# A squared-ReLU attention and mixer kernel: residual transposes moved in SyncE's queue, and two more x transposes on TensorE

## The chip, the cores and the metric

One NeuronCore of a Trainium2 chip runs the whole program. Five engines work beside each other and meet at semaphores: TensorE (PE in the profile; its weight loads are PEld), VectorE (DVE), ScalarE (ACT), GpSimd (POOL) and SyncE (SP), which here only issues DMAs. The metric is the device time of one execution in microseconds, the median over runs.

## The reference

```python
scores = scale * np.matmul(q, k.transpose(0, 1, 3, 2))      # q, k, v: 8 x 12 x 448 x 64
attn = np.maximum(scores, 0.0) ** 2 / S
attn_out = np.matmul(attn, v)
x = attn_out.transpose(0, 2, 1, 3).reshape(B, S, H * D)     # 8 x 448 x 768
xt = x.transpose(0, 2, 1)
h = np.maximum(xt @ w_tok1, 0.0) @ w_tok2                   # 448 -> 256 -> 448
u = x + h.transpose(0, 2, 1)
h2 = np.maximum(u @ w_ch1, 0.0) @ w_ch2                     # 768 -> 1536 -> 768
return u + h2
```

All inputs and the output are float32; the kernel computes in bfloat16 with float32 accumulation.

## The kernel before, in words

The 96 heads are taken in 24 groups of four (`ND`), three groups (`DB`) to a batch of the eight. For one group the work is:

- `load_four` brings q, k and v by DMA from GpSimd's queue (four buffers for each name); `transposes` turns q and k on TensorE (L141) and copies them to `qkT` (L155).
- `scores` multiplies for one of seven chunks of keys (L165); ScalarE applies ReLU into `at` (L174), and VectorE squares it (L181).
- `values` multiplies with v (L193); `values_out` scales the result into `xT` (L211), which has the model's channels on the partitions.
- `x_back` turns `xT` into `x_sb`, tokens on the partitions. It has two ways. For groups below `XDMA` it makes eight TensorE transposes into a PSUM buffer of the pool `ps_mm` (tag `bank`, two buffers; L237) and a copy (L246). From `XDMA` on it issues two DMA transposes on SP's queue (L229).
- `token1` and `token2` are the two token-mixing products (L255 with ReLU in L263, L278); VectorE adds `xT` and writes `uT_sb` (L286).
- `u_back` issues two DMA transposes on SP's queue that turn the group's part of `uT_sb` into `u_sb`, the residual with tokens on the partitions (L308). `u_sb` has three buffers, one for a batch.

When a batch's three groups are through, `channel_work` puts its channel mixing into a queue of units: twelve `channel1` units (six matmuls each, L320, with ReLU in L327) and two `channel2` units (twelve matmuls each, L359) for each output tile of 128 rows. The second of each pair of batches has four tiles, the first three; tiles are numbered t=0 to 6 over a pair. A `channel2` unit covers half of the 768 columns; VectorE adds `u_sb` to its result into `out_sb` (L366), and after the second half SP issues two DMAs to the output (L378). The `channel2` units of batch 0 are queued only with those of batch 1. All units take their PSUM from the same two `bank` buffers as `token1` and the TensorE form of `x_back`.

Groups 0 to 2 and the step of group 3 have a schedule written out by hand. From step i = 4 on, one loop holds the order: in step i, `scores` belong to group i, while `values`, `x_back`, `token1` and `token2` belong to group i-1, and `transposes` to group i+1. `fill` takes units from the queue by a credit of estimated cost. In each step, behind `x_back(i-1)`, comes the load of group i+3; if group i-1 is not below `XDMA`, a one-element GpSimd copy (`gate`, L537) that reads `x_sb` stands ahead of it in GpSimd's queue, so that the load waits until the DMA transposes have landed.

The order of the code is the order in each engine's queue; each queue runs in order, and semaphores hold an instruction until its operands are there.

Of the kernel before, what the change touches and what calls it, by code (L numbers as in the profile page):

```python
# [16 lines left out]
def kernel(  # L17
# [20 lines left out]
    DB = H // 4  # L38
# [78 lines left out]
    def load_wc2(i, parts):  # L117
        n = EC // parts
        nc.gpsimd.dma_start(
            out=wc2[:, i * n : (i + 1) * n, :],  # L120
            in_=moe_w_ch2.rearrange("(e p) n -> p e n", p=128)[:, i * n : (i + 1) * n, :],
        )
# [36 lines left out]
    def scores(i, c):  # L159
        sb = qkT[i]  # L160
        ps = ps_att.tile([128, 2, 512], FP32, tag="att", name="sc_ps")
        for r in range(2):
            for g in range(2):
                h = slice(64 * g, 64 * (g + 1))
                nc.tensor.matmul(  # L165
                    ps[64 * r : 64 * (r + 1), g, :S],
                    lhsT=sb[h, r, 1, c * 64 : (c + 1) * 64],
                    rhs=sb[h, r, 0, :],
                    start=True,
                    stop=True,  # L170
                    skip_group_check=True,
                )
        at = attn.tile([128, 2, S], BF16, name="at", bufs=12)
        nc.scalar.activation(at, ps[:, :, :S], AF.Relu)  # L174
        squares.append(at)
        at2[i, c] = at

    def square(keep=0):
        while len(squares) > keep:
            at = squares.pop(0)  # L180
            nc.vector.tensor_tensor(out=at, in0=at, in1=at, op=ALU.mult)  # L181

    def values(i, cs):
        v_raw = raws[i, "v"]
        if i not in accs:
            accs[i] = [ps_acc.tile([128, 512], FP32, tag=f"acc{r}", name="acc_ps") for r in range(2)]
        ps = accs[i]
        for c in cs:
            at = at2.pop((i, c))
            for r in range(2):  # L190
                for g in range(2):
                    h = slice(64 * r, 64 * (r + 1))
                    nc.tensor.matmul(  # L193
                        ps[r][64 * g : 64 * (g + 1), :S],
                        lhsT=v_raw[h, g, c, :],
                        rhs=at[h, g, :],
                        start=(c == 0),
                        stop=(c == QC - 1),
                        skip_group_check=True,
                    )  # L200

    def values_out(i, split=False):
        b, d = divmod(i, DB)
        ps = accs.pop(i)
        for r in range(2):
            if split and r == 1:
                nc.scalar.activation(
                    xT[b % 2][:, 2 * d + r, :S], ps[r][:, :S], AF.Copy, scale=float(alpha2)
                )
                continue  # L210
            nc.vector.tensor_scalar(  # L211
                out=xT[b % 2][:, 2 * d + r, :S],
                in0=ps[r][:, :S],
                scalar1=float(alpha2),
                scalar2=None,
                op0=ALU.mult,
            )


    x_tiles, r1_tiles, uT_tiles = {}, {}, {}  # L220
    XDMA = 6

    def x_back(i, place="bank", copy=None):
        b, d = divmod(i, DB)
        x_sb = mix.tile([128, 2, 4, 128], BF16, name="x_sb")
        x_tiles[i] = x_sb
        if i >= XDMA:
            for r in range(2):
                nc.sync.dma_start_transpose(  # L229
                    out=x_sb[:, r], in_=xT[b % 2][:, 2 * d + r, :]  # L230
                )
            return
        pool = ps_mm if place == "bank" else ps_acc
        ps = pool.tile([128, 2, 512], BF16, tag=place, name="x_ps")
        for r in range(2):
            for c in range(4):
                nc.tensor.matmul(  # L237
                    ps[:, r, c * 128 : (c + 1) * 128],
                    lhsT=xT[b % 2][:, 2 * d + r, c * 128 : (c + 1) * 128],
                    rhs=ident,  # L240
                    is_transpose=True,
                    start=True,
                    stop=True,
                    skip_group_check=True,
                )
        (copy or nc.vector.tensor_copy)(  # L246
            x_sb.rearrange("n r c d -> n (r c d)"), ps.rearrange("n r t -> n (r t)")
        )
# [17 lines left out]
    def token2(i, early=False, rs=(0, 1)):  # L266
        b, d = divmod(i, DB)
        if d == 0 and b % 2 == 0 and 0 in rs:
            uT_tiles[b // 2] = mix.tile([128, NP, 2 * S], BF16, name="uT_sb")
        r1 = r1_tiles[i]  # L270
        off = (b % 2) * S
        if early:
            parts = {r: ps_mm.tile([128, 512], FP32, tag="bank", name="h_ps1") for r in rs}
        else:
            parts = {r: ps_acc.tile([128, 512], FP32, tag=f"acc{r}", name="h_ps") for r in rs}
        for r in rs:
            for j in range(JC):
                nc.tensor.matmul(  # L278
                    parts[r][:, :S],
                    lhsT=r1[:, j, r * 128 : (r + 1) * 128],  # L280
                    rhs=wt2[:, j, :],
                    start=(j == 0),
                    stop=(j == JC - 1),
                )
        for r in rs:
            nc.vector.tensor_tensor(  # L286
                out=uT_tiles[b // 2][:, 2 * d + r, off : off + S],
                in0=parts[r][:, :S],
                in1=xT[b % 2][:, 2 * d + r, :S],
                op=ALU.add,  # L290
            )
        if 1 in rs:
            u_back(i)


    r2_tiles, u_tiles, out_tiles = {}, {}, {}

    def chunks(b):
        half = NT // 2
        return range(half) if b % 2 == 0 else range(half, NT)  # L300

    def u_back(i):
        b, d = divmod(i, DB)
        t = chunks(b)
        if d == 0:
            u_tiles[b] = mix.tile([128, NP, NT - NT // 2, 128], BF16, name="u_sb", bufs=3)
        for p in (2 * d, 2 * d + 1):
            nc.sync.dma_start_transpose(  # L308
                out=u_tiles[b][:, p, : len(t), :],
                in_=uT_tiles[b // 2][:, p, t.start * 128 : t.stop * 128],  # L310
            )
# [91 lines left out]
    def fill(share, least=0):  # L403
        if not queue:
            return
        credit[0] += share * rate[0]
        done = 0
        while queue and (credit[0] > 0 or done < least):
            cost, unit = queue.pop(0)
            credit[0] -= cost  # L410
            unit()
            done += 1
# [74 lines left out]
    i = DB  # L487
    square()
    values(i - 1, (4, 5, 6))
    values_out(i - 1, split=True)  # L490
    scores(i, 0)
    token2(i - 2, early=True)
    x_back(i - 1, place="acc0")
    scores(i, 1)
# [4 lines left out]
    square(keep=1)  # L499
    scores(i, 3)  # L500
    token2(i - 1, early=True)
    square(keep=1)
    scores(i, 4)
# [15 lines left out]
    for i in range(DB + 1, ND + 2):  # L519
        slow = i <= 2 * DB  # L520
        if i == 2 * DB + 1:
            rate[0] = (EC * C1 + NT * C2) / DB
        if i < ND:
            scores(i, 0)
            scores(i, 1)
        if 0 <= i - 1 < ND:
            values(i - 1, range(QC))
            values_out(i - 1)
        if i < ND:
            scores(i, 2)  # L530
        if slow:
            fill(1 / 3, least=1)
        if 0 <= i - 1 < ND:
            x_back(i - 1)
        if i + PRE < ND:
            if i - 1 >= XDMA:
                nc.gpsimd.tensor_copy(gate, x_tiles[i - 1][:1, 1, 3, 127:])  # L537
            load_four(i + PRE)
        if i == 5:
            load_wc2(1, 2)  # L540
        square()
        if not slow:
            fill(1 / 3)
        if i < ND:
            scores(i, 3)
            scores(i, 4)
        if i + 1 < ND:
            transposes(i + 1)
        square()
        if not slow:  # L550
            fill(2 / 9)
        if 0 <= i - 1 < ND:
            token1(i - 1)
        fill(1 / 3 if slow else 1 / 9, least=1)
        if i < ND:
            scores(i, 5)
            scores(i, 6)
        if 0 <= i - 1 < ND:
            token2(i - 1)
            if (i - 1) % DB == DB - 1:  # L560
                channel_work((i - 1) // DB)
        square()
        fill(1 / 3, least=1 if slow else 0)
# [32 lines left out]
```

## Time and profile before

| | |
|---|---|
| median of 13 runs | 386.4 us (383.56 to 392.57) |
| the profiled execution | 386.83 us, span 385.1 us |
| TensorE busy | 366.2 us (95%) |
| VectorE, ScalarE, GpSimd busy | 205.4, 213.2, 98.0 us |
| mean granted TensorE clock | 0.994 |
| DMA moved | 43.84 MB, mean 114 GB/s |
| `u_sb` transposes on SP's queue | 48, median 3.3 us to landing (2.3 to 13.0) |
| `x_sb` transposes on SP's queue | 36, median 2.4 us to landing (2.4 to 9.4) |
| `x_sb` by TensorE | 6 groups |

The span runs from the first to the last instruction; the time of the run lies a little above it. A row of the timeline gives the start, the duration, the engine, the line, the operation with its output and input, and in square brackets the idle time of the engine before it with what ended it. "SPq" rows are issues on SP's queue and not transfers; the transfer lands later. Busy time of TensorE is modelled, so the idle between its groups is the better guide.

### The profile page before, as it was taken

Reading aid. Unit: us, or ns where it says so; the run is one execution under the profiler, and the core shown is the slowest. Engines: PE = TensorE matmul, PEld = TensorE weight load, DVE = VectorE, ACT = ScalarE, POOL = GpSimd, SP = SyncE. Lnnn points to the kernel's source line nnn. Section 1 sums busy time; section 2 is a strip of 40 time slices with the busy share of each in tenths; the row PEclk is TensorE's granted clock in tenths of the full one; section 3 lists DMA queues with packets and bytes.
Section 4 is the critical chain, followed back from the end, with each engine's and each line's share of the span. In section 5 each row is a group of like instructions: output and inputs, shape, how many; then the busy total and the mean of one; then the engine's idle time right before and its main releaser. Section 6 shows DMA issues by size and latency. Waiting matters only on the chain.

```text
span 385.1 us, 10117 instructions
## 1 busy us (share of the span) xinstructions
PE 366.2 (95%) x4319; PEld 200.0 (52%) x4319; DVE 205.4 (53%) x369; ACT 213.2 (55%) x297; POOL 98.0 (25%) x176
## 2 busy tenths in 40 slices
PE   8888979959999999999999999999999999999995
PEld 3444535524555655555545655555555555555563
DVE  2785668842576665555654756545744755121022
ACT  4996868844653446764676455764576455411400
POOL 8973632603303303213214303213030000000000
PEclk9999999998999999999999999999999999999999
DMA  8999999996367897478566687467571433224024
GB/s 151 118 138 175 159 202 176 184 161 93 61 121 123 156 167 132 60 112 149 119 96 78 119 165 136 75 99 135 104 116 27 90 90 94 53 44 108 0 51 114
DMA packets 72014, 43.84 MB, mean 114 GB/s; under 512 B 46048, under 2 KB 68512, under 8 KB 71968
## 3 DMA queue, kind: packets, MB, share of 16 engines
q0 software_dynamic: 24416, 21.47, 40.2%
q1 hardware_dynamic: 47248, 21.28, 28.3%
q8 instruction: 34, 0.56, 0.6%
q10 hardware_dynamic: 304, 0.43, 0.4%
q14 instruction: 12, 0.10, 0.1%
HBM read 43.38 MB, written 11.01 MB: 141 GB/s over the span
## 4 chain that ended last, share of the span: by engine, by line
PE 81%; DMA 11%; POOL 3%; DVE 2%; ACT 2%; issue 1%; POOLq 0%; ACTq 0%
PE m_ps L359 28%; PE m_ps L320 26%; PE sc_ps L165 8%; PE acc_ps L193 7%; PE t_ps L255 5%; PE h_ps L278 4%; DMA wc<-in_moe_w_ch_dram 4%; DMA x_sb<-xT 3%; DMA k_raw<-in_k_dram 3%; PE qkT_ps L141 2%; ACT at L174 1%; POOL q_raw L83 1%; DVE at L181 1%; DMA wt<-in_moe_w_tok_dram 1%; POOL wt L96 1%
## 5 line engine op out<-in xcount | busy, mean ns | idle before, releaser
L174 ACT ACTIVATE at<-sc_ps 128x896 bf16<-128x896 f32 x168 | 145.1, 921 | 58.9 <-PE sc_ps L165 58.6
L320 PE MATMUL m_ps<-uT_sb,wc 128*128 128x448 bf16 x564 | 116.7, 355 | 2.4 <-DMA wc<-in_moe_w_ch_dram 2.2
L359 PE MATMUL m_ps<-wc,r_sb 128*128 128x384 bf16 x672 | 115.2, 326 | 0.0
L181 DVE TENSOR_TENSOR at<-at 128x896 bf16<-128x896 bf16 x168 | 97.3, 620 | 6.9 <-ACT at L174 6.9
L359 PEld LDWEIGHTS <-r_sb 128*128 128x128 bf16 x672 | 64.3, 98 | 45.6 <-issue 4.1
L327 ACT ACTIVATE r_sb<-m_ps 128x448 bf16<-128x448 f32 x94 | 51.1, 543 | 63.4 <-PE m_ps L320 62.9
L320 PEld LDWEIGHTS <-wc 128*128 128x128 bf16 x564 | 53.5, 98 | 52.9 <-issue 5.2
L366 DVE TENSOR_TENSOR out_sb<-m_ps,u_sb 128x384 f32<-128x384 f32 x56 | 31.1, 555 | 61.2 <-PE m_ps L359 60.2
L165 PE MATMUL sc_ps<-qkT 64*64 64x448 bf16 x672 | 52.7, 360 | 2.9 <-ACT at L174 2.3
L286 DVE TENSOR_TENSOR uT_sb<-h_ps,xT 128x448 bf16<-128x448 f32 x48 | 27.8, 618 | 47.6 <-PE h_ps L278 47.5
L211 DVE TENSOR_SCALAR xT<-acc_ps 128x448 bf16<-128x448 f32 x45 | 26.1, 619 | 37.3 <-PE acc_ps L193 37.3
L537 POOL COPY gate<-x_sb 1x1 bf16<-1x1 bf16 x14 | 3.2, 227 | 150.4 <-DMA x_sb<-xT 150.4
L193 PE MATMUL acc_ps<-at,v_raw 64*64 64x448 bf16 x672 | 38.6, 350 | 0.0
L83 POOL DMA_DIRECT2D q_raw<-in_q_dram x48 | 28.8, 611 | 18.2 <-DMA wc<-in_moe_w_ch_dram 13.0
L165 PEld LDWEIGHTS <-qkT 64*64 64x64 bf16 x672 | 15.6, 105 | 31.6 <-issue 27.6
L255 PE MATMUL t_ps<-x_sb,wt 128*128 128x256 bf16 x192 | 25.6, 277 | 6.4 <-DMA x_sb<-xT 5.7
L83 POOL DMA_DIRECT2D v_raw<-in_v_dram x48 | 29.4, 634 | 8.6 <-DMA wc<-in_moe_w_ch_dram 5.7
L155 DVE COPY qkT<-qkT_ps 128x896 bf16<-128x896 bf16 x39 | 22.5, 618 | 15.9 <-PE qkT_ps L141 15.9
L83 POOL DMA_DIRECT2D k_raw<-in_k_dram x46 | 28.0, 625 | 3.1 <-DMA q_raw<-in_q_dram 2.4
L263 ACT ACTIVATE r_sb<-t_ps 128x512 bf16<-128x512 f32 x24 | 14.3, 597 | 25.5 <-PE t_ps L255 25.4
L193 PEld LDWEIGHTS <-v_raw 64*64 64x64 bf16 x672 | 20.2, 107 | 12.1 <-issue 0.8
L255 PEld LDWEIGHTS <-wt 128*128 128x128 bf16 x192 | 18.4, 99 | 12.3 <-DMA x_sb<-xT 5.2
(38 smaller groups left out, 118.8 us busy)
## 6 DMA issues: line engine op xcount, KB each, us to landing
out_dram<-out_sb SPq DMA_DIRECT2D x54, 192.0 KB, 2.7
q_raw<-in_q_dram POOLq DMA_DIRECT2D x48, 112.0 KB, 4.2
v_raw<-in_v_dram POOLq DMA_DIRECT2D x48, 112.0 KB, 5.2
k_raw<-in_k_dram POOLq DMA_DIRECT2D x46, 112.0 KB, 4.7
wc<-in_moe_w_ch_dram POOLq DMA_DIRECT2D x4, 1152.0 KB, 13.2
u_sb<-uT_sb SPq DMA_TRANSPOSE x48, 3.3
x_sb<-xT SPq DMA_TRANSPOSE x36, 2.4
k_first<-in_k_dram SPq DMA_DIRECT2D x1, 224.0 KB, 3.5
```

The costliest lines, as they stand in the source:

```text
L83: eng.dma_start(out=dst[64 * r : 64 * (r + 1)].rearrange("p g c d -> p g (c d)"), in_=src[b, h0 : h0 + 2].rearrange("g (p c) d -> p g (c d ...
L165: nc.tensor.matmul(ps[64 * r : 64 * (r + 1), g, :S], lhsT=sb[h, r, 1, c * 64 : (c + 1) * 64], rhs=sb[h, r, 0, :], start=True, stop=True, s ...
L174: nc.scalar.activation(at, ps[:, :, :S], AF.Relu)
L181: nc.vector.tensor_tensor(out=at, in0=at, in1=at, op=ALU.mult)
L193: nc.tensor.matmul(ps[r][64 * g : 64 * (g + 1), :S], lhsT=v_raw[h, g, c, :], rhs=at[h, g, :], start=(c == 0), stop=(c == QC - 1), skip_gro ...
L211: nc.vector.tensor_scalar(out=xT[b % 2][:, 2 * d + r, :S], in0=ps[r][:, :S], scalar1=float(alpha2), scalar2=None, op0=ALU.mult,)
L255: nc.tensor.matmul(ps[:, j, :], lhsT=wt1[:, c, j * 128 : (j + 1) * 128], rhs=x_sb[:, :, c, :], start=(c == 0), stop=(c == 3),)
L286: nc.vector.tensor_tensor(out=uT_tiles[b // 2][:, 2 * d + r, off : off + S], in0=parts[r][:, :S], in1=xT[b % 2][:, 2 * d + r, :S], op=ALU.add,
L320: nc.tensor.matmul(ps[:, :S], lhsT=wc1[:, g, e * 128 : (e + 1) * 128], rhs=uT[:, g, off : off + S], start=(g == 0), stop=(g == CC - 1),)
L327: nc.scalar.activation(r2[:, e, off : off + S], ps[:, :S], AF.Relu)
L359: nc.tensor.matmul(ps[:, :HN], lhsT=r2[:, e, t * 128 : (t + 1) * 128], rhs=wc2[:, e, cols], start=(e == 0), stop=(e == EC - 1),)
L366: nc.vector.tensor_tensor(out=o[:, cols].rearrange("n (g d) -> n g d", d=128), in0=ps[:, :HN].rearrange("n (g d) -> n g d", d=128), in1=u_ ...
```

## The change

Three things are edited. `XDMA` goes from 6 to 8, so groups 6 and 7 (steps 7 and 8) are transposed on TensorE, and the loads of groups 10 and 11 have no gate ahead of them. `token2` no longer calls `u_back`, but puts the group on a list. And from step 7 on, the loop takes from this list behind `x_back(i-1)`: one group in step 7, up to two in each later step.

```diff
     x_tiles, r1_tiles, uT_tiles = {}, {}, {}
-    XDMA = 6
+    XDMA = 8
...
         if 1 in rs:
-            u_back(i)
+            u_later.append(i)
...
     r2_tiles, u_tiles, out_tiles = {}, {}, {}
+    u_later = []
...
         if 0 <= i - 1 < ND:
             x_back(i - 1)
+        if i > 2 * DB:
+            for _ in range(1 if i == 2 * DB + 1 else 2):
+                if u_later:
+                    u_back(u_later.pop(0))
         if i + PRE < ND:
```

The list thus gives group 0 in step 7, groups 1 and 2 in step 8, 3 and 4 in step 9, 5 and 6 in step 10, 7 and 8 in step 11, 9 and 10 in step 12, and one group in each step after that. In SP's queue, the transposes of `u_sb` for group i-2 now come behind those of `x_sb` for group i-1, where before they came ahead of them.

## The prediction

> **What bounds the kernel now.** I read the page first: engine shares, slices.
>
> ```profile
> PE 366.2 (95%) x4319; PEld 200.0 (52%) x4319; DVE 205.4 (53%) x369; ACT 213.2 (55%) x297; POOL 98.0 (25%) x176
> ...
> DMA  8999999996367897478566687467571433224024
> ```
>
> TensorE is busy for 366.2 of 385.1 us; no other engine passes 55%. A change pays where TensorE idles, and costs where it adds TensorE work or a new wait. The DMA engines are full for the first nine slices of 9.6 us. Next, the table of waits.
>
> ```profile
> POOL gate L537 <- DMA x_sb<-xT: 150.4, 14, 12.5
> DVE out_sb L366 <- PE m_ps L359: 60.2, 30, 15.0
> PE t_ps L255 <- DMA x_sb<-xT: 5.7, 2, 4.8
> ```
>
> The gate's 150 us is GpSimd pacing loads; nobody computing waits for it. TensorE waits twice for a DMA transpose of x, 5.7 us in all. No DVE wait for `u_sb` appears: every `u_sb` was early. The timeline shows the long wait, in step 7. (Steps are known by their two `xT` evictions on DVE: 76.16 in step 7, 97.34 in 8, 112.05 in 9, 126.29 in 10.)
>
> ```profile
> 75.95 0.36 PE L165 MATMUL sc_ps<-qkT 64*64 64x448 bf16 x4
> 76.16 1.16 DVE L211 TENSOR_SCALAR xT<-acc_ps 128x448 bf16<-128x448 f32 x2 [1.20 <-PE acc_ps L193]
> 76.84 4.68 SPq L229 DMA_TRANSPOSE x_sb<-xT  x2
> 86.86 1.66 PE L255 MATMUL t_ps<-x_sb,wt 128*128 128x256 bf16 x8 [4.82 <-DMA x_sb<-xT]
> 88.32 2.39 PE L320 MATMUL m_ps<-uT_sb,wc 128*128 128x448 bf16 x6
> 90.64 0.57 PE L165 MATMUL sc_ps<-qkT 64*64 64x448 bf16 x8
> ```
>
> The first x transpose issues at 76.84, the pair lands at 86.8. The matmuls after the idle are slow: eight L255 in 1.66 us against 1.03 in step 9, six L320 in 2.39 against 1.31. The table of windows says why (busy columns, then granted clock 0.56):
>
> ```profile
> 86.80:90.70 3.90, 3.83 (x18) 1.92 (x22) 0.00 (x0) 0.60 (x1) 3.72 (x7) 0.56 0.63 73
> ```
>
> Last, step 10, where the put-off transposes will matter:
>
> ```profile
> 126.29 1.16 DVE L211 TENSOR_SCALAR xT<-acc_ps 128x448 bf16<-128x448 f32 x2 [1.27 <-PE acc_ps L193]
> 126.98 2.88 SPq L229 DMA_TRANSPOSE x_sb<-xT  x2
> 128.97 0.55 DVE L366 TENSOR_TENSOR out_sb<-m_ps,u_sb 128x384 f32<-128x384 f32 x1
> 131.37 2.12 PE L359 MATMUL m_ps<-wc,r_sb 128*128 128x384 bf16 x12
> 134.38 2.11 PE L359 MATMUL m_ps<-wc,r_sb 128*128 128x384 bf16 x12
> ```
>
> The DVE row at 128.97 is the second half of output tile t=3, the first tile of batch 1 (the `out_sb` rows run t=0 at 104.08 and 106.91, t=1 at 110.22 and 114.72, t=2 at 117.43 and 121.15, t=3 at 124.47 and 128.97).
>
> **What the Trainium skill says.** "TensorE: Matmul & The Clock Gate", Part 1, says that a whole idle window of about 3.4 us halves TensorE's clock, that a similar time of work restores it, and that the window runs freely. The trace agrees: after 4.82 us idle the clock was 0.56 for about 3.9 us; after 2.2 us idle at 51.8 six L320 still took 1.31. The same page (Architectural detail) calls DVE and ACT strict FIFO, so one late operand holds everything behind it on DVE. "DMA: Bandwidth & Descriptors", Issuing engines are not separate DMA queues, says that transfers of all issuers interleave on the same 16 engines; the x pair of step 7 took 8.3 and 9.4 us beside loads, 2.4 and 2.5 in step 8.
>
> **Part 1: PE transposes in steps 7 and 8.** Step 7: the model is the same operation in step 6 (xT ready at 67.68, x transposes 67.75 to 68.36, copy 68.40 to 69.09). Scores end at 76.31; the second xT is ready at 77.32. The first four transposes fit before it; the last four (half of 0.61) end at about 77.7. L320 x12, at 76.24 before, then starts 1.4 late. From there without the DMA wait: 2.4 (L320 x12) + 1.0 (scores and attention transposes) + 2.4 (L320 x12) + 1.0 (L255 x8) + 1.2 (L320 x6) = 8.0, so scores at 85.6 against 90.64: a gain of 5.0, of which about 1.7 is the cold clock (0.6 + 1.1). The x copy ends near 78.5, well before L255 at 83.4. Step 8: token1 had no wait there, so the 1.4 is pure cost. The two DVE copies (0.69 each) come out of DVE's idle (3.39 before the step 8 eviction; without that cover they would cost 1.4 in all).
>
> **Part 2: two gates fewer.** The loads of groups 10 and 11 no longer wait at 86.8 and 101.9, but follow the loads of group 9 (until 74.3), held only by their buffers. They meet the second half of `wc` in the full DMA time; it was issued at 69.05, the slowest `wc` landing took 18.0, and it is first needed at about 97. Worth nothing; if late, a microsecond or two.
>
> **Part 3: the residual transposes.** The built program shows that the six of batch 0 are not put off in time. They stand at the head of SP's queue, each waiting only for its own DVE add (issues from 25.18 to 40.0, as before). Only batch 1's six move: SP's order is now output t=0, x of group 8, u of groups 3 and 4, outputs t=1 and t=2, x of group 9, u of group 5, u of group 6. So the crowding up to 52 us stays; what leaves is the six transposes issued from 52.4 to 75.9. The `wc` wait that ends at 54.05 began at 51.8, before them, and from 54 to 76 TensorE was busy 21.78 of 22.0 us: worth nothing. In step 9 the wait of 0.83 (L255 at 118.13) should mostly vanish, since group 11's loads are no longer there: 0.6 (0 to 0.8).
>
> Step 9's new demand: t=3's first half (124.47) needs u of group 3 and half of 4. After x at 112.73, with 1.25 an issue, the third u transpose starts at 117.7; even at a landing of 5.2 (the u pair at 122.93) that is 122.9. In time, with a microsecond to spare.
>
> Step 10 is late. u of group 5 stands behind x of group 9: x issues 126.98 to about 129.6, its first u to 130.85, its second starts there and lands 2.3 (least) to 5.2 later. I take 2.8, the load of group 13 being gated still: 133.65. DVE wanted it at 128.97. Behind it in DVE's FIFO are t=4's first half, two qkT copies, two squares, and t=4's second half; TensorE has two `bank` buffers, filled with t=3 and t=4, and stops at 131.37. DVE then needs 0.05 + 0.56 + 0.56 + 1.15 + 1.15 + 0.56 = 4.0 until the buffer for t=5 is free, at 137.7; TensorE wrote t=5 at 134.38 before. Cost 3.3; bounds 2.8 and 5.7. TensorE's own idle there is 134.25 - 131.37 = 2.9, below the window; at landings over 3.4 us it can reach it, and adds up to 1.7.
>
> Later batches: u comes some 5 us later than before (from the end of a step to behind x in the next), but twelve `m_ps` L320 units (1.14 each, so 13.7 us) precede each batch's output tiles. Nothing.
>
> **Sum.** -5.0 + 1.4 - 0.6 + 3.3 = -0.9 us. Against the profiled execution (span 385.1, time 386.83) that is 385.9; it is 0.4 above the median of 386.4, so I predict 385.5 as the median. A change within 0.5% (1.9 us) can't be told from none: the forecast is "same", leaning to faster.
>
> **Rivals.** (1) The new stall hides: if the u of group 5 is early or DVE's wait doesn't reach TensorE, -5.0 + 1.4 - 0.6 = -4.2 gives 382.2. For: the wait is DVE's, which idles 2.2 us soon after; against: two buffers only, DVE in order. (2) Slower: the step 10 stall at its upper price plus a cold clock, 5.7 + 1.7, and nothing from step 9: +3.5, about 390. It decides (above 388.3) once the stall costs more than 6.1 with its cold clock, that is, a landing over about 4 us that also makes an idle window. For: u took 5.2 at 122.93; against: no loads are due at 131. (3) Step 7's stall in the trace is longer than usual, as a cold clock hangs on the window's phase: without it the gain is 3.3, and the sum +0.8, about 387.2. (4) The change doesn't do what it says: true of batch 0, but inside the likeliest case.
>
> **Chances.** Likeliest case 0.45 (its own range 384.5 to 387), hidden stall 0.22, slower 0.16, weaker gain 0.17. For 8 in 10 the range leaves out the far ends of (1) and (2): 382.7 to 388.6. Faster takes most of (1) and the lower edge of the likeliest: 0.30. Slower takes (2) and a little of (3): 0.19. Within: 0.51.
>
> **What would show it.** Right: no DMA wait before L255 in steps 7 to 9; an L237 group in steps 7 and 8 with about 1.1 us idle; no clock dip there; a new DVE wait for `u_sb` in step 10, of about 4.7 us, and a TensorE wait for `out_sb`'s buffer of about 3; u of batch 0 still issued from 25 us. Wrong: a DVE wait for `u_sb` at t=3's first half, a TensorE wait for `wc` or `k_raw` in steps 7 to 9, or no TensorE idle in step 10.

## The result, and the profile after

The changed kernel takes 388.28 us in the median (11 runs), the kernel before 385.88 in the runs beside it (48); the ratio is 1.0089, with a 95% interval from 1.0058 to 1.012. It is slower by 0.9%, some 3.4 us. This ratio leaves out slow runs, more than 1.5% above the fastest of the same kernel, and these are 14 of the 48 before and none after; the medians of all runs lie 2.4 us apart. The forecast was 385.5 us and no measurable change.

The page of the changed kernel, the shares and the DMA row as before, with the row of the granted clock:

```profile
PE 368.5 (95%) x4335; PEld 201.7 (52%) x4335; DVE 206.5 (53%) x371; ACT 213.1 (55%) x297; POOL 96.8 (25%) x174
...
PEclk9999999999999699999999999999999999999999
DMA  8999999941169939589367587549361254323023
```

The clock dips in one slice, the fourteenth (125 to 135 us). In the trace before, the dip was in the tenth. The table of waits (four of its rows):

```profile
DVE out_sb L367 <- PE m_ps L360: 62.1, 30, 15.0
DVE out_sb L367 <- DMA u_sb<-uT_sb: 5.5, 2, 5.2
PE m_ps L360 <- DVE out_sb L367: 3.5, 1, 3.5
PE t_ps L255 <- DMA x_sb<-xT: 1.5, 2, 1.1
```

The long DMA wait for x is gone, and two rows are new: VectorE waits 5.2 us for `u_sb` in step 10 (and once more, 0.28 us, in step 9, which TensorE doesn't feel), and TensorE 3.5 us for the VectorE operation that waited. Step 7 in the timeline:

```profile
73.95 1.15 DVE L211 TENSOR_SCALAR xT<-acc_ps 128x448 bf16<-128x448 f32 x2 [1.20 <-PE acc_ps L193]
74.64 0.93 PE L237 MATMUL x_ps<-ident,xT 128*128 128x128 bf16 x8 [0.53 <-DVE xT L211]
75.60 0.69 DVE L246 COPY x_sb<-x_ps 128x1024 bf16<-128x1024 bf16 x1 [0.49 <-PE x_ps L237]
...
81.03 1.04 PE L255 MATMUL t_ps<-x_sb,wt 128*128 128x256 bf16 x8
81.90 1.30 PE L321 MATMUL m_ps<-uT_sb,wc 128*128 128x448 bf16 x6
```

L255 follows without a wait, at the full clock (1.04 us for eight against 1.66). Step 10, where the time goes:

```profile
120.40 1.15 DVE L211 TENSOR_SCALAR xT<-acc_ps 128x448 bf16<-128x448 f32 x2 [1.09 <-PE acc_ps L193]
121.09 2.51 SPq L229 DMA_TRANSPOSE x_sb<-xT  x2
123.65 5.82 SPq L309 DMA_TRANSPOSE u_sb<-uT_sb  x4
128.39 1.02 DVE L367 TENSOR_TENSOR out_sb<-m_ps,u_sb 128x384 f32<-128x384 f32 x2 [5.23 <-DMA u_sb<-uT_sb]
129.00 4.00 PE L360 MATMUL m_ps<-wc,r_sb 128*128 128x384 bf16 x12 [3.45 <-DVE out_sb L367]
```

The u transposes of group 5 are issued at 123.65 behind x of group 9. VectorE, which had squared until 123.16, waits until 128.39; TensorE stops for 3.45 us. Twelve L360 then take 4.00 us instead of 2.11. The table of windows shows the clock. Its last three columns are the granted clock (0.52 in the first row), the DMA share and GB/s; ahead of them stand the busy times of PE, PEld, DVE, ACT and POOL:

```profile
128.90:134.80 5.90, 5.80 (x22) 3.23 (x22) 3.19 (x7) 0.00 (x0) 2.01 (x4) 0.52 1.13 199
134.80:141.00 6.20, 6.20 (x60) 3.25 (x62) 3.34 (x6) 2.98 (x4) 0.00 (x0) 1.00 0.26 69
```

From one `xT` eviction to the next the steps took (us):

| | before | after | difference | predicted |
|---|---|---|---|---|
| step 7 (76.16 / 73.95) | 21.18 | 15.88 | -5.30 | -5.0 |
| step 8 | 14.71 | 16.06 | +1.35 | +1.4 |
| step 9 | 14.24 | 14.51 | +0.27 | -0.6 |
| step 10 | 15.38 | 21.44 | +6.06 | +3.3 |
| sum | | | +2.38 | -0.9 |
| from there to the end of the span | 243.39 | 244.57 | +1.18 | 0 |

The two spans differ by only 1.3 (386.4 and 385.1), because step 7 came 2.2 us later in the trace before, after its `wc` wait. That wait, a long start, comes and goes between executions and isn't the change's: five of the thirteen traces of this case have it (1.85 to 3.54 us, with step 7 some 2 to 5.6 us late), and a second trace of the kernel before doesn't, with step 7's eviction at 74.08. From step 7 on the table gives +3.6 in all; against the second trace of the kernel before it is +2.7.

### The profile page after: what moved, and what is told of

It reads as the page before. It is cut to its first block, busy times and chain, and to the rows that moved or that the text cites. A ratio compares the mean times of both kernels' runs of the same rounds, so it can differ in the third digit from the quotient of the medians.

```text
span 386.4 us, 10103 instructions
## 1 busy us (share of the span) xinstructions
PE 368.5 (95%) x4335; PEld 201.7 (52%) x4335; DVE 206.5 (53%) x371; ACT 213.1 (55%) x297; POOL 96.8 (25%) x174
## 4 chain that ended last, share of the span: by engine, by line
PE 84%; DVE 6%; DMA 4%; ACT 3%; issue 1%; SPq 1%; POOL 0%; POOLq 0%; DVEq 0%; ACTq 0%
PE m_ps L360 27%; PE m_ps L321 26%; PE sc_ps L165 9%; PE acc_ps L193 8%; PE t_ps L255 6%; PE h_ps L278 5%; ACT at L174 3%; PE qkT_ps L141 2%; DMA x_sb<-xT 2%; DVE xT L211 2%; DVE at L181 1%; DVE uT_sb L286 1%; DMA q_raw<-in_q_dram 1%; DMA u_sb<-uT_sb 1%; PE m_ps L339 1%
## 5 line engine op out<-in xcount | busy, mean ns | idle before, releaser
L360 PE MATMUL m_ps<-wc,r_sb 128*128 128x384 bf16 x672 | 117.2, 330 | 3.5 <-DVE out_sb L367 3.5
L360 PEld LDWEIGHTS <-r_sb 128*128 128x128 bf16 x672 | 65.1, 99 | 50.0 <-issue 9.0
L542 POOL COPY gate<-x_sb 1x1 bf16<-1x1 bf16 x12 | 2.1, 177 | 140.8 <-DMA x_sb<-xT 140.8
L255 PE MATMUL t_ps<-x_sb,wt 128*128 128x256 bf16 x192 | 25.8, 279 | 2.2 <-DMA x_sb<-xT 1.5
L255 PEld LDWEIGHTS <-wt 128*128 128x128 bf16 x192 | 18.6, 100 | 8.5 <-issue 3.9
```

What stands on the lines that cost most here:

```text
L255: nc.tensor.matmul(ps[:, j, :], lhsT=wt1[:, c, j * 128 : (j + 1) * 128], rhs=x_sb[:, :, c, :], start=(c == 0), stop=(c == 3),)
L360: nc.tensor.matmul(ps[:, :HN], lhsT=r2[:, e, t * 128 : (t + 1) * 128], rhs=wc2[:, e, cols], start=(e == 0), stop=(e == EC - 1),)
```

## The experiments

Two theories stood against each other. A: the loss is the late u of group 5 in step 10 with the cold clock behind it. B: the TensorE transposes cost more than they save. A third (C) spreads the loss over all moved transposes.

**One part alone: the TensorE transposes.** The kernel before, with one line changed.

```diff
-    XDMA = 6
+    XDMA = 8
```

> Only the TensorE transposes of groups 6 and 7 (and so two gates fewer); the u transposes stay where they were before. Theory A (the loss is the late u of group 5 in step 10, with the cold clock that follows): no DVE wait for u_sb and no TensorE idle in step 10; step 7 takes about 16 us from xT to xT instead of 21, step 8 about 16 instead of 14.7; 4 us below before, ratio about 0.990. Theory B (the TensorE transposes cost more than they save, because the DMA wait of step 7 is usually short): ratio 1.00 or above.

Measured: 381.42 us (12 runs), ratio 0.9907 (0.9873 to 0.994). Step 7 took 15.88, step 8 16.06, step 10 15.22, no wait for `u_sb`, clock 0.998. B falls: this half of the change gains about 3.6 us. Once more, beside the gate experiment below:

> TensorE transposes of groups 6 and 7 alone, once more, beside the kernel with the gates kept: 381.4 again, ratio about 0.991, and 16 us from xT to xT in step 7.

381.06 us, ratio 0.9879 (0.984 to 0.9918), step 7 again 15.88.

**The other part alone: the put-off u transposes.** The changed kernel with `XDMA = 6`.

> Only the moved u transposes; x of groups 6 and 7 by DMA as before. Theory A: the late u of group 5 is there, DVE waits about 5 us for it in step 10 and TensorE about 3.5, with a cold clock after it; about 6 us above before, ratio about 1.015, less what the DMA wait of step 7 loses with the u of groups 4 and 5 out of its way (up to 5). Theory B: the moved transposes cost nothing, ratio 1.00 or below.

Measured: 387.66 us, ratio 1.0094 (1.0064 to 1.0123). The waits, longest first:

```profile
DVE out_sb L367 <- DMA u_sb<-uT_sb: 14.6, 3, 6.8
PE m_ps L360 <- DVE out_sb L367: 4.6, 1, 4.6
```

VectorE waits three times for `u_sb`: 6.77 us in step 8 (for t=0), 1.77 in step 9 and 6.04 in step 10. SP's queue in this kernel, against the changed one below it, says why:

```profile
74.51 3.56 SPq L229 DMA_TRANSPOSE x_sb<-xT  x2
78.11 2.56 SPq L309 DMA_TRANSPOSE u_sb<-uT_sb  x2
89.02 2.50 SPq L229 DMA_TRANSPOSE x_sb<-xT  x2
91.57 6.80 SPq L309 DMA_TRANSPOSE u_sb<-uT_sb  x4
```

```profile
0.74 0.76 SPq L83 DMA_DIRECT2D k_first<-in_k_dram  x1
25.37 16.13 SPq L309 DMA_TRANSPOSE u_sb<-uT_sb  x6
101.33 1.16 SPq L379 DMA_DIRECT2D out_dram<-out_sb  x2
```

With x of group 6 in the queue, batch 0's u really is put off, until step 7 and 8. In the changed kernel nothing stands ahead of it, and its six transposes issue from 25.37, as before. The two parts of the change thus aren't a sum: the first keeps the second from moving batch 0's u. In this trace x of group 6 landed in 2.5 to 3.6 us and step 7 had no wait; but its loads of group 9 were also issued by 67 instead of 74, so that alone doesn't say which of the two cured it.

**Group 5 ahead of x of group 9.** The changed kernel, with three groups taken off the list in step 9.

```diff
-            for _ in range(1 if i == 2 * DB + 1 else 2):
+            for _ in range({7: 1, 9: 3}.get(i, 2)):
```

> The changed kernel, but step 9 takes three groups off the list, so that u of group 5 stands ahead of x of group 9 instead of behind it. Theory A: its two transposes land before 126, DVE doesn't wait for u_sb in step 10, the clock stays full, and the 6 us of step 10 are back: ratio to before about 0.992. Theory B, and any theory that puts the loss on the order of u behind x in all later steps: as the changed kernel, about 1.009.

Measured: 382.20 us, ratio 0.994 (0.9918 to 0.9963). No VectorE wait for `u_sb`, step 10 in 15.22, clock 0.998. The row that had waited follows the squares at once:

```profile
121.56 1.69 DVE L181 TENSOR_TENSOR at<-at 128x896 bf16<-128x896 bf16 x3
123.16 0.55 DVE L367 TENSOR_TENSOR out_sb<-m_ps,u_sb 128x384 f32<-128x384 f32 x1
```

Nearly all of the loss is back.

**Only group 5 late.** The TensorE transposes, and of all u transposes only group 5's moved. The diff is against the kernel of the first experiment.

```diff
         if 1 in rs:
-            u_back(i)
+            if i == 5:
+                u_later.append(i)
+            else:
+                u_back(i)
...
             x_back(i - 1)
+        if i == 10:
+            while u_later:
+                u_back(u_later.pop(0))
```

> TensorE transposes of groups 6 and 7, and of all u transposes only those of group 5 moved, from the end of step 6 to behind x of group 9 in step 10. Theory A (group 5 alone makes the loss): DVE waits about 5 us for u_sb in step 10, the clock dips, and the time is 6 us above the kernel with the TensorE transposes alone, ratio to before about 1.006. Theory C (the moved order of all groups adds up to the loss): within 2 us of the kernel with the TensorE transposes alone, ratio about 0.993.

Measured: 388.28 us, ratio 1.008 (1.0051 to 1.011), the changed kernel's own median. Its step 10:

```profile
121.19 2.67 SPq L229 DMA_TRANSPOSE x_sb<-xT  x2
...
123.91 2.57 SPq L312 DMA_TRANSPOSE u_sb<-uT_sb  x2
...
129.71 1.02 DVE L370 TENSOR_TENSOR out_sb<-m_ps,u_sb 128x384 f32<-128x384 f32 x2 [6.45 <-DMA u_sb<-uT_sb]
...
130.32 4.00 PE L363 MATMUL m_ps<-wc,r_sb 128*128 128x384 bf16 x12 [4.68 <-DVE out_sb L370]
```

The same place, a wait of 6.45 us instead of 5.23, and the same twelve slow matmuls; step 10 took 22.81. Two DMA instructions in one wrong place make the whole loss: the late u of group 5 is both necessary (the experiment before) and, beside the TensorE transposes, sufficient (this one), and C falls.

**The cold clock on its own.** The changed kernel, with nine matmuls of zeros in the idle of step 10. They are added work; their PSUM buffer is read by nobody.

```diff
             transposes(i + 1)
+        if i == 10:
+            busy = ps_att.tile([128, 2, 512], FP32, tag="att", name="busy_ps")
+            for m in range(9):
+                nc.tensor.matmul(busy[:, 0], lhsT=warm[:, :128], rhs=warm, start=True, stop=True)
```

> The changed kernel with nine matmuls of zeros (128x512, about 2 us) put into the idle of step 10, behind the attention transposes; they write a PSUM buffer that nobody reads. Theory A, with the cold clock as its second half: DVE's wait and TensorE's resumption stay at the same place, but twelve L360 behind it take 2.1 us instead of 4.0 and eight L255 1.0 instead of 1.9; 2.7 us below the changed kernel, ratio to before about 1.002. If the slow matmuls have another cause: ratio about 1.009 and the same slow rows.

```profile
130.44 2.10 PE L557 MATMUL busy_ps<-warm 128*128 128x512 bf16 x9 [0.35 <-ACT at L174]
...
132.53 1.02 DVE L367 TENSOR_TENSOR out_sb<-m_ps,u_sb 128x384 f32<-128x384 f32 x2 [4.83 <-DMA u_sb<-uT_sb]
133.14 2.11 PE L360 MATMUL m_ps<-wc,r_sb 128*128 128x384 bf16 x12 [0.60 <-DVE out_sb L367]
...
135.09 1.04 PE L255 MATMUL t_ps<-x_sb,wt 128*128 128x256 bf16 x8
```

VectorE still waits 4.83 us, but the matmuls behind it run at full speed. Step 10 took 18.55 instead of 21.44: in the traces 2.9 of its 6.06 us are the clock, and the 3.2 that stay are the stall itself. The time agrees in direction and is less sharp: 385.73 us, ratio 1.005 (1.0021 to 1.0078) against 1.0089, some 1.5 us, with intervals that overlap.

**The gates.** The TensorE transposes alone, with the gates of groups 6 and 7 kept.

```diff
-            if i - 1 >= XDMA:
+            if i - 1 >= 6:
```

> TensorE transposes of groups 6 and 7 with the u transposes as before, and the two gates of groups 6 and 7 kept ahead of the loads of groups 10 and 11; they now wait for the DVE copy of x. If the two gates are worth nothing: within 1 us of the same kernel without them (repeated beside it), ratio about 0.991. If the earlier loads help or harm: 1 to 3 us off in either direction.

Measured: 381.43 us against 381.06 beside it, ratio to before 0.9889 (0.9847 to 0.9931). The gates are worth nothing that these runs can tell, as forecast.

**Is step 7's wait usual?**

> The kernel before, unchanged, for a second trace. If the DMA wait of step 7 is usual: 3 us or more of TensorE idle ahead of L255 in step 7 and 19 us or more from xT to xT. If the first trace was an outlier: under 1.5 us of idle and no clock dip.

```profile
85.42 1.86 PE L255 MATMUL t_ps<-x_sb,wt 128*128 128x256 bf16 x8 [5.45 <-DMA x_sb<-xT]
87.08 2.21 PE L320 MATMUL m_ps<-uT_sb,wc 128*128 128x448 bf16 x6
```

One execution, 385.58 us; 21.84 from eviction to eviction. Both traces of the kernel before have the wait, so the prediction's third rival (a wait longer than usual in the trace) falls.

**Toward a better kernel.** Three variants of the kernel before, none of which moves group 5's u behind x of group 9.

> The kernel before with group 6 alone transposed on TensorE; group 7 keeps its DMA transposes, which landed in 2.4 us before. If step 7's wait was the whole gain and step 8's TensorE transposes pure cost (16.06 us from xT to xT against 14.71): 1.3 us below the kernel with both, ratio to before about 0.987. If the DMA x of group 7 comes late with the loads earlier: 0.991 or above.

`XDMA = 7`: 380.01 us, ratio 0.989 (0.9836 to 0.9944). Step 8 took 14.70 again, 1.36 less than with TensorE.

> Group 6 alone on TensorE, with its transposes put behind the two channel1 units of the step instead of ahead of them, so that TensorE doesn't wait for the xT eviction. If the wait was 0.6 to 1.0 of the 1.4 us that a step's TensorE transposes cost: 0.7 us below the kernel with group 6 ahead of the units, ratio about 0.985. If the later copy delays DVE's squares: no gain.

```diff
-    XDMA = 6
+    XDMA = 7
...
-        if 0 <= i - 1 < ND:
+        if 0 <= i - 1 < ND and i != 7:
             x_back(i - 1)
...
         if not slow:
             fill(1 / 3)
+        if i == 7:
+            x_back(i - 1)
```

378.95 us, ratio 0.9835 (0.979 to 0.988): the lowest median, below both kernels, though these runs can't tell it from the next variant. In its trace L237 takes 0.61 us with no wait in front, and step 7 14.97 against 15.88. (The traced execution had the long start, so its span of 382.5 is above the median.)

> The kernel before with one change of order in SP's queue: u of groups 4 and 5 is issued in step 7 behind x of group 6, which stays a DMA transpose; nothing on TensorE. If the u transposes of groups 4 and 5 (landings of 6 to 11 us) are what makes x of group 6 late: it lands in about 3 us, step 7 takes 14.5 us instead of 21, ratio about 0.985. If the loads make it late: x lands in 8 us as before, ratio 0.998 to 1.0.

```diff
-            u_back(i)
+            if i in (4, 5):
+                u_later.append(i)
+            else:
+                u_back(i)
...
             x_back(i - 1)
+        if i == 7:
+            while u_later:
+                u_back(u_later.pop(0))
```

379.1 us, ratio 0.9857 (0.9807 to 0.9906), with nothing on TensorE at all. The size came as expected; the trace shows only half of the reason:

```profile
84.48 1.03 PE L255 MATMUL t_ps<-x_sb,wt 128*128 128x256 bf16 x8 [2.79 <-DMA x_sb<-xT]
```

In this execution (382.75 us, with the long start; the other five took 378.49 to 379.51) x of group 6 still landed only after 6.6 to 7.4 us. The wait is 2.79 instead of 4.8 or 5.4, and the clock stays full, L255 in 1.03. That speaks for u of groups 4 and 5 as one part of step 7's wait, and for the loads in flight as another; no run here takes the two apart, and the traced execution isn't the typical one.

## Why the prediction was wrong

- **What bounds the kernel, and step 7 (-5.0): right.** -5.30 measured; step 7 took the same 15.88 in two traces of the kernel with the TensorE transposes alone.
- **Step 8 (+1.4): right**, +1.35. The kernel with group 6 alone gives it back (14.70), and in step 7 the placing behind the units saved 0.9 us, which was TensorE's wait for the eviction.
- **The gates (0) and batch 0's u (not moved in time): right**, the second visible in SP's queue from 25.37.
- **Step 9 (-0.6): wrong, by 0.9.** The wait I put down to group 11's loads stayed without them: TensorE waits 1.11, as x's second transpose landed in 4.2 us (4.0 before). Its cause is open.
- **Step 10 (+3.3): the step that failed.** The place, the waiter, the queue behind it and the two buffers were as described, but the term was mis-sized, +6.06, because it put the cold clock behind the stall at nothing. The stall itself was priced about right: with the clock kept full step 10 cost 3.2 (the first u issue took 1.52 us there). The second u transpose was issued 5.2 us after the eviction began, not 4.6, since the first one's issue took 1.91 and not 1.25; it landed in 2.65, near the 2.8 assumed. So TensorE idled 3.45 instead of 2.9, and the clock halved: 2.8 us more by the slow rows (4.00 - 2.11 and 1.91 - 1.04), 2.9 by the experiment. I had left this out of the sum, because the Trainium skill ("TensorE: Matmul & The Clock Gate", Part 1) gives a whole idle window of about 3.4 us for it, and had sized it at 1.7 at most from step 7's slow phase. Here the measurements decide against "whole". In the traces' record the clock changes only at the edges of windows of 3.41 us, and in the changed kernel 2.22 us of idle in one window (124.35 to 127.77) were enough; so the 2.9 I forecast was already in danger, depending on where the edge fell. And the half clock lasted two windows (6.83 us, from 127.77), where step 7's had lasted one (3.41 us, from 87.11): the first of the two still held 1.23 us of idle. The last section has the count.
- **Step 9's slack: gone.** I had given t=3's first half a microsecond to spare. The third u transpose was issued 7.0 us into the step instead of 5.7 and took 5.7 to land instead of 5.2, and VectorE did wait 0.28 for it, a sign I had named; it cost TensorE nothing.
- **Later batches (0): right for the steps.** Steps 11 to 23 took the same to within 0.2 us each in all thirteen traces, with u behind x or ahead of it. The 1.2 us of the table lie behind the last eviction: 0.6 by the end of the last matmul, with TensorE waiting 0.41 for x of group 23, and 0.6 after it (0.25 in the kernels with the TensorE transposes alone). Neither was followed.
- **The rivals.** What came is nearest to rival (2), given 0.16: the stall with a cold clock behind it. Step 10 cost 6.06, at the 6.1 from which I let it decide and under its full price of 7.4 (with nothing from step 9 that price makes +3.8, not the +3.5 of its sum; and 6.1 counts the 0.6 of step 9, without which the edge is 5.5). I tied it to a landing over 4 us, where half a microsecond more in SP's queue and the place of a window's edge did it. (1) and (3) are refuted, the first by the changed kernel's wait rows, the third by the second trace.

The sum with the measured step 10 and step 9 is -5.0 + 1.4 + 0.3 + 6.1 = +2.8. With a forecast so near zero, the one term that left out the clock decided the sign.

## What to carry to other kernels

A DMA that is put off has a deadline: find its first reader, what stands ahead in the issuing queue at that moment, and what waits behind the reader on its in-order engine; one pair of transposes behind one other pair cost 6 us here. Price a TensorE stall of about 2 us or more with a chance of half clock behind it: here, where it came in steps 7 and 10, that added another 1.7 to 2.9 us, and a few matmuls of zeros in the gap avoided it. And moving an instruction later in the code doesn't delay it when nothing ahead in its own queue has to wait.

## What the runs showed of the hardware

In all thirteen traces the changes of the granted clock lie whole multiples of 3.41 us apart. I cut each trace into windows of that length, counted from its first change, and added up TensorE's idle in each, up to its last matmul:

| clock in the window | TensorE idle in it (us) | windows | clock in the next window |
|---|---|---|---|
| full | 1.93 to 3.41 | 9 | half |
| full | 0 to 1.65 | 1396 | full |
| half | 0.92 to 3.33 | 4 | half |
| half | 0 to 0.45 | 9 | full |

So what counts here isn't the length of an idle but how much of it falls into one window. Idles of 2.22 us (the kernel before, ending at 54.05) and 2.79 us (u behind x of group 6) lay across an edge, with at most 1.41 in either window, and the clock stayed full. One of 2.38 us (the kernel with the gates kept) had 1.93 in one window, and the clock halved. One of 1.86 in step 8 of the kernel with only the u transposes put off halved it too, with 2.02 of idle in its window in all. Where the limit lies between 1.65 and 1.93 isn't shown, and TensorE's busy time is modelled.

- Nine matmuls of zeros, 2.1 us of work in a gap of 3.05 us, left at most 0.60 us of idle in a window, and the clock stayed full.
- Issuing one of these DMA transposes takes SP 1.2 to 1.3 us in most cases, and now and then more: the first u behind a pair of x took 2.42 and 1.91 us in steps 9 and 10 of the changed kernel, but 1.26 or 1.27 in all four such places of the kernel with only the u transposes put off. A pair of x and a pair of u behind it kept SP for 5.1 to 6.3 us in steps 7 to 10, and what stands behind them waits for that as well as for its own landing.
